# Filler products ahead of and between TensorE's first steps, a rebuilt order search, and a longer run of second stages at the end

## The chip, the cores and the metric

The kernel runs on one core of a Trainium2 chip. The metric is the device time of one execution in microseconds (us). The kernel before was timed in three runs: median 622.8 us, from 619.92 to 622.96.

## What is computed

Attention with a sliding window of 128 positions and 4 sink positions for 4 batches, 8 heads, 768 positions and a head width of 64, and behind it one feed-forward block over the 3072 tokens (512 to 2048 to 512, ELU between).

```python
keep = (pos[None, :] < n_sink) | ((rel >= 0) & (rel < window))
a = softmax(where(keep, scale * q @ k.T, -1e9)); attn = a @ v
x = attn.transpose(0, 2, 1, 3).reshape(B * S, H * D)   # 3072 x 512
h = x @ w_in                                            # 3072 x 2048
g = where(h > 0, h, exp(minimum(h, 0)) - 1)
return g @ w_out                                        # 3072 x 512
```

## The kernel before

The tokens are cut into nine chunks (`SIZES`, line 42) of two or three tiles of 128. Of each chunk the attention is computed first (`attention_f32`, line 545, for chunks 0 and 1 in 32-bit floats; `attention`, line 676, for the others), then the feed-forward block in 16 steps f (`feed_forward`, line 866). Numbers that need it are carried as two 16-bit halves, high and low.

A step f of a chunk has a **first stage** on TensorE (PE): 12 matmuls into one of two PSUM banks h (line 883). Then come an exponential on ScalarE (ACT, line 891), two operations on VectorE (DVE, lines 893 and 896), the high half on ACT (line 897) and the low half on GpSimd (POOL, line 902) or, for chunk 0, on DVE (line 899). The **second stage** on PE takes both halves: three matmuls for each of the chunk's tiles (line 913) into the accumulators. The high and low halves `gh` and `gl` have three buffers each (ring `gh`), so the buffer of step f is written again by step f + 3.

In the attention, scores of two heads (line 586) go through DVE (line 593: mask and row minimum) and ACT (line 596: exponential and sum), are turned on PE (line 603), copied to SBUF by ACT or DVE (line 607), multiplied with the values on PE (lines 644 and 652) and scaled by ACT and DVE (lines 665 to 669). Meanwhile the weights are fetched in 32 pieces and split into halves (lines 325 to 331, 488, 489).

Nothing of this order is left to the tile framework. Every step is a `Task` with an engine, a duration, dependencies and, on PE, a position `pos`. `Plan.order` (line 140) works out due times backwards from the PE positions (`backward`), lets each engine take in simulated time what is ready, PE by position and the others by due time (`forward`), and replays that order five times with small disturbances (`replay`). It does so 64 times, from the fourth on with due times shifted at random by up to 1 us, and keeps the order whose replays end first. `spare` (line 109) adds 1.2 us of slack to every result that another engine hands to a PE task at position 60 or later. A position counts half steps: chunk 8, the last one, begins at 256, and the end (`start`, line 1017) is 288. The plan's end is the end of the last PE task. `keep_order` writes the instructions in the order found; each engine then runs its own in that order.

At the end, the steps f = 13, 14 and 15 of chunk 8 have their second stages split by tile and put behind the last first stage (line 918): the last first stage has position 284.8 (line 886), the second stage of f = 12 has 285. A check follows: DVE reduces the sums of all exponentials (line 1015; the last two steps' at lines 1007 and 1008), PE spreads the result with one matmul at position 286 (line 1017), DVE makes a flag of it (line 1012). Each engine loads the flag (line 1264) and branches on it (line 1265): past a general path, normally not run, to the code that moves the last accumulators out (lines 1273 and 1275) and stores them (line 1276).

At the start, ACT fetches the four words of the scalars, DVE turns them into two numbers (lines 1227 to 1233), and one tiny PE product spreads these over the partitions (line 1234), from which DVE makes the masks.

Of the kernel before, what the change touches and what calls it, by code (L numbers as in the profile page):

```python
# [12 lines left out]
BF16 = mybir.dt.bfloat16  # L13
# [7 lines left out]
P = 128  # L21
B, H, S, D = 4, 8, 768, 64
DM, FF = 512, 2048
# [3 lines left out]
NF = FF // P  # L27
NW = 2 * NF
NS = 4
KW = NS + P  # L30
# [13 lines left out]
HALF = NF // 2  # L44
PARTS = [(0, 0, HALF), (1, 0, HALF), (0, HALF, NF), (1, HALF, NF)] + [(c, 0, NF) for c in range(2, len(SIZES))]
LAG = 2
NEAR = 1
WHOLE = 3
TURNED = 2
# [48 lines left out]
class Plan:  # L98
# [5 lines left out]
    LOADED = 4.3  # L104
    PATIENCE, LEEWAY, ISSUED = 0.1, 5.0, 0.15
    SWITCH = 0.096
    SPARE, SPARE_FROM = 1.2, 60

    def spare(self, t, u):
        return self.SPARE if u.eng == "PE" and t.eng != "PE" and u.pos >= self.SPARE_FROM else 0.0  # L110

    def __init__(self):
        self.tasks, self.rings = [], {}
# [1 line left out]
    def add(self, eng, dur, fn, *args, deps=(), lat=0.0, pos=None, or_=(), gap=2.0, port=None, mode=None):  # L115

        t = Task(eng, dur, fn, args, deps, lat, pos, gap, port, mode)
        for way in or_:
            t.ways[way[0]] = way[1:]
        self.tasks.append(t)  # L120
        return t

    def ring(self, name, writers, users, at=None):

        r = self.rings.setdefault(name, [])
        r.append((writers, users, len(r) if at is None else at))
# [13 lines left out]
    def order(self):  # L140
        self.link()
        pe = sorted((t for t in self.tasks if t.eng == "PE"), key=lambda t: (t.pos, t.n))
        clock = 0.0
        for t in pe:
            t.start = clock
            clock += t.dur
        best, dice = None, random.Random(0)
        for k in range(64):
            self.backward()
            for t in self.tasks:  # L150
                t.due += dice.uniform(-1.0, 1.0) if k >= 3 else 0.0
            self.forward()
            self.tasks.sort(key=lambda t: t.n)
            for i, t in enumerate(sorted(self.tasks, key=lambda t: (t.start, t.n))):
                t.turn = i
            found = [(t.turn, t, t.eng) for t in self.tasks]
            ends = [self.replay(random.Random(i)) for i in range(4)] + [self.replay()]
            end = sum(ends) / len(ends)
            if best is None or end < best[0]:
                best = end, found, {t: t.start for t in self.tasks}  # L160
        self.end = best[0]
        for _, t, e in best[1]:
            t.take(e)
            t.start = best[2][t]
        return [t for _, t, _ in sorted(best[1], key=lambda v: v[0])]

    def replay(self, dice=None):

        order = {e: [] for e in self.HOP}
        for t in sorted(self.tasks, key=lambda t: t.turn):  # L170
            order[t.eng].append(t)
        for e in order:
            order[e].reverse()
        left = {t: len(t.deps) for t in self.tasks}
        ready = dict.fromkeys(self.tasks, 0.0)
        free, dma, lock, mode, last = dict(self.BEGIN), self.LOADED, 0.0, None, 0.0
        for _ in self.tasks:
            _, e = min((max(free[e], ready[o[-1]]), e) for e, o in order.items() if o and not left[o[-1]])
            t = order[e].pop()
            s = max(free[e], ready[t])  # L180
            if e == "PE":
                s, mode = s + (self.SWITCH if t.mode != mode else 0.0), t.mode
                last = s + t.dur
            if t.shares(e):
                s = max(s, lock)
                lock = s + t.dur
            t.start = s
            free[e] = s + t.dur + (0.05 if e == "POOL" else 0.0)
            f = s + t.dur + self.HOP[e]
            if t.lat:  # L190
                dma = max(s + t.dur, dma) + t.lat
                f = dma + t.gap + (dice.choice((-0.5, -0.5, 0.0, 0.5, 1.5)) if dice else 0.0)
            elif dice and e != "PE":
                free[e] += t.dur * dice.uniform(0.0, 0.04)
            for u in t.succ:
                ready[u] = max(ready[u], f if e != "PE" or u.eng != e else s + t.dur)
                left[u] -= 1
        return last
# [183 lines left out]
def fast_path(tc, ctx, first, kq, vx, wt, out, nw, inside, flag, limits):  # L382
# [56 lines left out]
    def slot(name):  # L439
        turn[name] = turn.get(name, -1) + 1  # L440
        return turn[name] % RINGS[name]
# [98 lines left out]
                later.append((writer, us))  # L540
        x_old.append((lo, hi, users))

    later, po_users = [], []

    def attention_f32(c):

# [129 lines left out]
    def attention(c):  # L676
# [10 lines left out]
        def split_keys(h):  # L687


            st = kqs[slot("kqs")]  # L690
            buf = kqr[slot("kq")] if c >= WHOLE else None
            o, kw = KQ_OFF[c, h], kc + qc
            if c < WHOLE:
                ld = None
                if (c, h) not in first["kq"]:
                    ld = add("SP", 0.45, lambda: nc.sync.dma_start(st[:, :kw], kq[:, o : o + kw]), lat=dma_us(P * kw * 4))
                users = []
                return st, None, ld, ld, users
            raw, hi = st[:, :kw], buf[:, :kw]
            ld = None  # L700
            if (c, h) not in first["kq"]:
                ld = add("SP", 0.45, lambda: nc.sync.dma_start(raw, kq[:, o : o + kw]), lat=dma_us(P * kw * 4))
            th = add("ACT", act_us(kw), lambda: nc.scalar.activation(hi, raw, AF.Copy, scale=KQ_SCALE), deps=[ld])  # L703

            lo = buf[:, KQ_MAX : KQ_MAX + kc]
            tk = add("DVE", dve_us(kc), lambda: nc.vector.scalar_tensor_tensor(lo, raw[:, :kc], KQ_SCALE, hi[:, :kc], ALU.mult, ALU.subtract), deps=[th], port=True)
            tl = add("DVE", dve_us(qc), lambda: nc.vector.scalar_tensor_tensor(hi[D:, kc:], raw[D:, kc:], KQ_SCALE, hi[D:, kc:], ALU.mult, ALU.subtract), deps=[th], port=True)  # L707
            users = []
            ring("kqs", [ld or th], [th, tk, tl])
            ring("kq", [th], users)  # L710
            return hi, lo, tk, tl, users

        def taken_values(p, val, prods, v_users, po):
# [152 lines left out]
    def feed_forward(c, f0, f1, start):  # L866
# [4 lines left out]
        for f in range(f0, f1):  # L871
            hp = h_ps[slot("h")]
            gf = gs[slot("g")][:, :n]
            i = slot("gh")
            gh, gl = ghs[i], gls[i]

            def stage1(hp=hp, f=f):
                win = w[2 * f].rearrange("p t (a f) -> p t a f", a=ND)
# [36 lines left out]

            deps = [th, tl, *w_done[2 * f + 1], *(evacs[:nt] + (po_users if c == len(SIZES) - 1 else []) if f == f0 else s2)]
            at2 = start + 2 * (f - f0) + 1 + 2 * LAG
            if c == len(SIZES) - 1 and f >= f1 - 3:

                if len(s2) < nt:  # L920
                    s2 = s2 * nt
                at2 = [start + 2 * (f1 - 1 - f0) + (0.5 + 0.01 * i if f == f1 - 1 else 0.1 * i + 0.01 * f) + (0.0 if i < nt - 1 else 1.0) for i in range(nt)]
                s2 = [add("PE", 3 * 0.216, stage2([(k, i) for k in range(3)]), deps=[th, tl, *w_done[2 * f + 1], s2[i]], pos=at2[i]) for i in range(nt - (f == f1 - 1))] + s2[nt - (f == f1 - 1) :]
                if f == f1 - 1:
                    for e, end in enumerate(ends):
                        s2[-1] = add("PE", 3 * (0.162, 0.057)[e], stage2([(k, nt - 1) for k in range(3)], parts=[end]), deps=[th, tl, *w_done[2 * f + 1], s2[-1]], pos=at2[-1] + 0.001 * e)
            elif f < f1 - 1:
                s2 = [add("PE", 3 * nt * 0.216, stage2([(k, i) for k in range(3) for i in range(nt)]), deps=deps, pos=at2)]
            else:

                s2 = [add("PE", 3 * 0.216, stage2([(k, i) for k in range(3)]), deps=deps, pos=at2 + 0.01 * i) for i in range(nt)]
            ring("g", [a], [b] if near else [th, tl])
            ring("gh", [th], s2)
        for i in range(nt if c < len(SIZES) - 1 else 0):
            rows_ = out[r0 + i * P : r0 + (i + 1) * P, :]
            if f1 < NF:
# [77 lines left out]
    sp = s_ps[len(s_at) % RINGS["s"]]  # L1014
    a = add("DVE", 1.45, in_range, deps=[*seen, *exps_done[:-2], limits_])
    a = add("DVE", 0.2, last_in_range, deps=[a, *exps_done[-2:]])
    b = add("PE", 0.1, lambda: nc.tensor.matmul(sp[:, 0:3], ones, some16, start=True, stop=True), deps=[a], pos=start - 2.0)
    ring("s", [b], [add("DVE", 0.16, decide, deps=[b])], len(s_at))
    for writer, users in later:
        writer.deps.extend(users)  # L1020
    tasks = plan.order()
    if VERBOSE:
        plan.report()
    keep_order(tc, tasks, first["spread"])


VERBOSE = False
# [186 lines left out]
def attention_moe(tc, kq, vx, words_in, wt, out):  # L1214
    nc = tc.nc
    with ExitStack() as ctx:
# [14 lines left out]
        nc.vector.tensor_scalar(nw1, low, 0.0, None, ALU.is_lt)  # L1231
        nc.vector.tensor_tensor(nw1, nw1, high, ALU.add)
        nc.vector.scalar_tensor_tensor(nw1, nw1, 4294967296.0, low, ALU.mult, ALU.add)
        spread = nc.tensor.matmul(last_acc[:, 0:2], ones1, nw1, start=True, stop=True).ins
        nc.vector.tensor_copy(nw, last_acc[:, 0:2])

# [7 lines left out]

        widths = {"kqs": KQ_MAX, "vs": (NK_MAX + 1) * P}
        first = {n: [pool.tile([P, w], F32, name=f"{n}{i}") for i in range(RINGS[n])] for n, w in widths.items()}
        first["spread"] = spread
        first["kq"], first["vs_"] = {(0, 0), (0, 2)}, {(0, 0)}
        nk, qc = len(key_tiles(CHUNKS[0])), len(CHUNKS[0]) * P
        for n, i, src, o, w in (  # L1250
# [50 lines left out]
```

## Time and profile before

| | |
|---|---|
| runs | 619.92, 622.80, 622.96 us |
| profiled execution | 622.7 us |
| its span, first to last instruction | 620.8 us |
| what lies around the span | 1.9 us |
| PE busy | 603.3 us, 97% of the span |
| DVE, ACT, POOL busy | 77%, 70%, 42% |

Every row is of the one profiled execution. Times in a row count from the span's start. A busy share is that of an engine's instructions; register loads, branches and waits are not in it. In a timeline row the bracket says how long the engine had been idle and what released it; in a row of waits, engine, tile and line stand left of the arrow, what was waited for stands right of it, and then come total us, times and the longest. The letter q behind an engine (PEldq) means its sequencer.

### The profile page before, as it was taken

To read this page: it belongs to the slowest core of one execution; us is meant where nothing else is said; L and a number is where in the kernel's file an instruction comes from. 1 tells how busy PE (TensorE), PEld (TensorE's weight loads), DVE (VectorE), ACT (ScalarE), POOL (GpSimd) and SP (SyncE) were. 2 spreads that over 40 slices of the span, in tenths; PEclk is the share of its full clock that TensorE was granted. 3 is DMA by queue.
4 is the path that set the end of the run, shared out by engine and by line. 5 is a ranking of instruction groups with operands and counts; after the bars stand their busy time and mean duration, and the time that the engine had idled before them with its cause. 6 is when DMAs were issued, how large, how long until landed. Compare 5 with 4: busy or idle time off the path is not lost. (4 is left out here: it accounts for less than half of the span.)

```text
span 620.8 us, 13588 instructions
## 1 busy us (share of the span) xinstructions
PE 603.3 (97%) x4587; PEld 365.8 (59%) x4587; DVE 477.8 (77%) x1284; ACT 435.8 (70%) x1236; POOL 262.2 (42%) x510
## 2 busy tenths in 40 slices
PE   7799999999999999999999999999999999999994
PEld 5576666567766565555555565655555565555552
DVE  7899889979989787787788987887888987433231
ACT  5899999877888786776777777766776776332221
POOL 2678787534344434332334444232434443212221
PEclk9899999999999999999999999999999999999998
DMA  8576876939878565483957948586756935410001
GB/s 308 193 285 249 246 230 206 225 93 213 214 172 215 147 156 124 114 212 79 201 134 199 203 105 161 131 225 127 203 130 152 239 49 133 97 52 1 1 0 57
DMA packets 117359, 97.53 MB, mean 157 GB/s; under 512 B 88994, under 2 KB 94370, under 8 KB 117282
## 3 DMA queue, kind: packets, MB, share of 16 engines
q1 hardware_dynamic: 117136, 96.53, 60.8%
q8 instruction: 38, 0.62, 0.4%
q14 instruction: 39, 0.32, 0.2%
q10 hardware_dynamic: 146, 0.07, 0.0%
HBM read 67.99 MB, written 7.34 MB: 121 GB/s over the span
## 5 line engine op out<-in xcount | busy, mean ns | idle before, releaser
L883 PE MATMUL h<-x,w 128*128 128x384 f16 (+1 forms) x1728 | 271.9, 308 | 1.1 <-DVE gl L899 1.0
L883 PEld LDWEIGHTS <-w 128*128 128x128 f16 x1728 | 167.4, 98 | 88.7 <-issue 3.1
L902 POOL TENSOR_TENSOR gl<-g,gh 128x384 f16<-128x384 f32 (+1 forms) x128 | 114.4, 895 | 190.9 <-ACT gh L897 161.0
L913 PE MATMUL acc<-w,gh 128*128 128x512 f16 x576 | 164.6, 379 | 0.1
L913 PEld LDWEIGHTS <-gh 128*128 128x128 f16 x800 | 75.8, 98 | 70.4 <-issue 1.6
L891 ACT ACTIVATE g<-h 128x384 f32<-128x384 f32 (+1 forms) x144 | 64.4, 448 | 71.4 <-PE h L883 61.9
L897 ACT ACTIVATE gh<-g 128x384 f16<-128x384 f32 (+1 forms) x128 | 62.6, 490 | 54.2 <-DVE g L896 53.8
L813 DVE SCALAR_TENSOR_TENSOR pq<-e,st,pq 128x256 f16<-128x256 f32 x160 | 85.5, 560 | 19.7 <-ACT pq L812 18.9
L800 ACT ACTIVATE e<-e,st 128x264 f32<-128x264 f32 x160 | 78.1, 489 | 17.5 <-DVE st L798 17.2
L913 PE MATMUL acc<-w,gl 128*128 128x512 f16 x288 | 87.8, 379 | 0.0
L893 DVE TENSOR_SCALAR g<-g 128x384 f32<-128x384 f32 (+1 forms) x96 | 36.7, 382 | 62.7 <-ACT g L891 61.7
L812 ACT ACTIVATE pq<-e,st 128x256 f16<-128x256 f32 x160 | 70.8, 483 | 8.0 <-DVE st L805 4.5
L896 DVE SCALAR_TENSOR_TENSOR g<-g,h 128x384 f32<-128x384 f32 (+1 forms) x128 | 65.8, 514 | 5.4 <-ACT g L893 4.4
L913 PE MATMUL last_acc<-w,gh 128*128 128x512 f16 (+1 forms) x192 | 69.9, 370 | 0.0
L798 DVE CUSTOM_DVE_ANT_0 e<-s,m 128x264 f32<-128x264 f32 x160 | 61.0, 404 | 11.2 <-PE s L777 10.8
L913 PEld LDWEIGHTS <-gl 128*128 128x128 f16 x400 | 38.5, 98 | 44.5
L804 POOL TENSOR_SCALAR st<-st 128x2 f32<-128x2 f32 x80 | 20.9, 261 | 85.2 <-ACT e L800 81.4
L703 ACT ACTIVATE kq<-kqs 128x780 f16<-128x780 f32 (+1 forms) x48 | 42.7, 897 | 10.5 <-PE s L777 8.1
L489 POOL TENSOR_TENSOR w<-wv,w 128x512 f16<-128x512 f32 x32 | 38.9, 1223 | 5.7 <-ACT w L488 4.6
L776 PE MATMUL s<-kq 128*128 128x264 f16 (+1 forms) x144 | 35.5, 267 | 0.5 <-DVE kq L707 0.5
L777 PE MATMUL s<-kq 128*128 128x264 f16 (+1 forms) x144 | 35.5, 267 | 0.0
L913 PE MATMUL last_acc<-w,gl 128*128 128x512 f16 (+1 forms) x96 | 35.5, 370 | 0.0
(152 smaller groups left out, 817.0 us busy)
## 6 DMA issues: line engine op xcount, KB each, us to landing
raw<-in_wt_dram SPq DMA_DIRECT2D x32, 512.0 KB, 5.1
kqs<-in_kq_dram SPq DMA_DIRECT2D x24, 456.0 KB, 3.5
kqs<-in_kq_dram SPq DMA_DIRECT2D x24, 390.0 KB, 3.4
qk<-in_kq_dram SPq DMA_DIRECT2D x48, 195.0 KB, 4.6
out_dram<-wv SPq DMA_DIRECT2D x21, 256.0 KB, 4.5
vs<-in_vx_dram SPq DMA_DIRECT2D x20, 256.0 KB, 3.1
vm<-in_vx_dram SPq DMA_DIRECT2D x6, 768.0 KB, 5.8
vs<-in_vx_dram SPq DMA_DIRECT2D x12, 320.0 KB, 3.9
```

Source lines behind the costliest of these rows:

```text
L489: tl = add("POOL", 1.16, lambda: nc.gpsimd.tensor_tensor(w[k][:, 1, :], v, w[k][:, 0, :], ALU.subtract), deps=[th])
L703: th = add("ACT", act_us(kw), lambda: nc.scalar.activation(hi, raw, AF.Copy, scale=KQ_SCALE), deps=[ld])
L798: red = add("DVE", 0.08 + 0.00104 * wd, lambda ee=ee, me=me, sp=sps[e], m=m, wd=wd: nc.vector.tensor_tensor_reduce(ee, sp[:, :wd], m[:, :w ...
L800: ex = add("ACT", act_us(wd, sums=True), lambda ee=ee, me=me, rs=rs[:, e : e + 1]: nc.scalar.activation(ee, ee, AF.Exp, bias=me, scale=-1. ...
L812: a = add("ACT", act_us(nb * P, True), lambda src=src, hi=hi, re=re: nc.scalar.activation(hi, src, AF.Copy, scale=re), deps=[rr])
L813: b = add("DVE", dve_us(nb * P) + 0.03, lambda src=src, hi=hi, lo=lo, re=re: nc.vector.scalar_tensor_tensor(lo, src, re, hi, ALU.mult, ALU ...
L883: nc.tensor.matmul(hp[:, :n], win[:, part, d, :], xx[:, :n], start=k == 0, stop=k == 3 * ND - 1)
L891: a = add("ACT", act_us(n) + 0.06, lambda gf=gf, hp=hp, sums=sums: nc.scalar.activation(gf, hp[:, :n], AF.Exp, scale=1.0 / G_SCALE, accum_ ...
L896: b = add("DVE", dve_us(n) - 0.035, lambda gf=gf, gd=gd, hp=hp: nc.vector.scalar_tensor_tensor(gd, gf, 0.0, hp[:, :n], ALU.min, ALU.max), ...
L897: th = add("ACT", act_us(n) - (0.03 if near else 0.0), lambda gd=gd, gh=gh: nc.scalar.activation(gh[:, :n], gd, AF.Copy), deps=[b])
L902: tl = add("POOL", pool_us(n), lambda gl=gl, gd=gd, gh=gh: nc.gpsimd.tensor_tensor(gl[:, :n], gd, gh[:, :n], ALU.subtract), deps=[th])
L913: nc.tensor.matmul(to[:, : cols.stop - cols.start], gg[:, i * P : (i + 1) * P], wout[:, part, cols], start=f == f0 and k == 0, stop=f == f ...
```

## The change

It has four parts. (1) Nine matmuls of 248 columns of ones go to PE ahead of the scalars' spreading product (`EARLY`). (2) After the plan is made, each PE task that the plan starts before 28 us gets such matmuls in front of it, as many as fit the gap that the plan has between it and the PE task before, less 0.2 us, at 0.11 us each; nobody reads their results. The first PE task gets one. (3) The search takes 250 trials instead of 64; from the fourth on a trial starts from the best due times so far and shifts those of one stretch of 25 us that reaches over a gap of PE. The plan's end also counts the flag's end plus 4.5 us (`JUMP`). (4) In chunk 8 the slack of 1.2 us is no longer given from position 274 on; the second stage of f = 12 is split by tile and put behind the last first stage like those of f = 13 to 15, its halves held in two buffers of the keys and queries (`kqr`) that are free by then; the check's matmul has position 285 instead of 286.

```diff
+EARLY, WARM_UNTIL = 9, 28.0
...
-    SPARE, SPARE_FROM = 1.2, 60
+    SPARE, SPARE_POS = 1.2, (60, 2 * NF * len(SIZES) - 14)
+    JUMP = 4.5
     def spare(self, t, u):
-        return self.SPARE if u.eng == "PE" and t.eng != "PE" and u.pos >= self.SPARE_FROM else 0.0
+        return self.SPARE if u.eng == "PE" and t.eng != "PE" and self.SPARE_POS[0] <= u.pos < self.SPARE_POS[1] else 0.0
...
-        for k in range(64):
-            self.backward()
+        for k in range(250):
+            if k < 3:
+                self.backward()
+                due = {t: t.due for t in self.tasks}
+            else:
+                a = dice.choice(best[4]) + dice.uniform(-25.0, -5.0)
+                size = dice.choice((0.5, 1.5, 4.0))
+                due = {t: d + (dice.uniform(-size, size) if a < t.start < a + 25.0 else 0.0) for t, d in best[3].items()}
             for t in self.tasks:
-                t.due += dice.uniform(-1.0, 1.0) if k >= 3 else 0.0
+                t.due = due[t]
...
+    def waits(self):
+        pe = sorted((t for t in self.tasks if t.eng == "PE"), key=lambda t: t.start)
+        return [b.start for a, b in zip(pe, pe[1:]) if b.start - a.start - a.dur > 0.25]
...
+            if not t.succ and e == "DVE":
+                last = max(last, f + self.JUMP)
...
-            i = slot("gh")
-            gh, gl = ghs[i], gls[i]
+            held = c == len(SIZES) - 1 and f == f1 - 4
+            if held:
+                gh, gl = kqr[0][:, :TOK_MAX], kqr[1][:, :TOK_MAX]
+            else:
+                i = slot("gh")
+                gh, gl = ghs[i], gls[i]
...
-            if c == len(SIZES) - 1 and f >= f1 - 3:
+            if c == len(SIZES) - 1 and f >= f1 - 4:
...
-            ring("gh", [th], s2)
+            if held:
+                th.deps.extend(u for us in kq_users[-2 * RINGS["kq"] :] for u in us)
+            else:
+                ring("gh", [th], s2)
...
-    b = add("PE", 0.1, lambda: nc.tensor.matmul(sp[:, 0:3], ones, some16, start=True, stop=True), deps=[a], pos=start - 2.0)
+    b = add("PE", 0.1, lambda: nc.tensor.matmul(sp[:, 0:3], ones, some16, start=True, stop=True), deps=[a], pos=start - 3.0)
...
+    pe = sorted((t for t in tasks if t.eng == "PE" and t.start < WARM_UNTIL), key=lambda t: t.start)
+    pe[0].fn = filled(pe[0].fn, first["warm"], h_ps[1], 1)
+    for a, b in zip(pe, pe[1:]):
+        b.fn = filled(b.fn, first["warm"], s_ps[1] if a.start > 7.0 else h_ps[1], int((b.start - a.start - a.dur - 0.2) / 0.11))
     keep_order(tc, tasks, first["spread"])
+
+def filled(fn, warm, to, n):
+    def run(*args):
+        for _ in range(n):
+            warm(to)
+        fn(*args)
+    return run
...
+        ones_k, ones_n = (nc.const_aps.tensor(1.0, [P, n], BF16) for n in (P, DM - 2 * KW))
+        def warm(to):
+            nc.tensor.matmul(to[:, 2 * KW :], ones_k, ones_n, start=True, stop=True)
+        for _ in range(EARLY):
+            warm(last_acc)
         spread = nc.tensor.matmul(last_acc[:, 0:2], ones1, nw1, start=True, stop=True).ins
```

## Rows read from the trace of the kernel before

**Rows 1.** The page, part 1: busy time of each engine over the span.
```profile
PE 603.3 (97%) x4587; PEld 365.8 (59%) x4587; DVE 477.8 (77%) x1284; ACT 435.8 (70%) x1236; POOL 262.2 (42%) x510
```

**Rows 2.** Busy time by stretch: PE, PEld, DVE, ACT, POOL, clock, DMA share, GB/s.
```profile
8.00:12.00 4.00, 4.00 (x27) 3.11 (x27) 3.16 (x16) 2.89 (x10) 0.57 (x3) 1.00 1.01 393
...
16.00:20.00 4.00, 2.16 (x14) 1.17 (x10) 4.00 (x15) 3.32 (x14) 2.34 (x4) 0.85 0.68 261
20.00:24.00 4.00, 3.88 (x32) 2.63 (x28) 2.68 (x10) 3.01 (x8) 1.51 (x4) 0.72 0.01 2
...
32.00:48.00 16.00, 15.78 (x149) 11.09 (x147) 14.89 (x44) 15.74 (x47) 11.85 (x20) 1.00 0.81 286
...
64.00:128.00 64.00, 62.29 (x466) 40.21 (x467) 56.94 (x140) 57.55 (x168) 44.77 (x71) 1.00 0.84 232
128.00:256.00 128.00, 128.00 (x1039) 81.55 (x1037) 106.34 (x300) 101.48 (x299) 51.14 (x116) 1.00 0.68 160
```

**Rows 3.** Waits of PE over the whole span.
```profile
PE last_acc L1234 <- DVE one_row L1233: 2.7, 1, 2.7
PE h L603 <- ACT e L596: 1.8, 1, 1.8
...
PE h L883 <- DVE gl L899: 1.0, 2, 0.7
```

**Rows 4.** Timeline of PE, first 30 us: start, duration, line, tiles, shape, count.
```profile
7.47 1.54 PE L603 MATMUL h<-ident,e 128*128 128x128 f32 x6
...
12.36 0.87 PE L603 MATMUL h<-ident,e 128*128 128x128 f32 x6
...
19.32 1.25 PE L586 MATMUL s<-kqs 64*128 64x264 f32 x4
...
23.16 0.72 PE L586 MATMUL s<-kqs 64*128 64x264 f32 x4
...
29.26 1.47 PE L883 MATMUL h<-x,w 128*128 128x256 f16 x12
```

**Rows 5.** Waits of DVE that PE ended, first 30 us.
```profile
DVE pt L607 <- PE h L603: 2.4, 3, 1.2
...
DVE e L593 <- PE s L586: 1.3, 3, 0.6
```

**Rows 6.** Timeline of the last 20 us, all engines.
```profile
603.12 0.59 PE L913 MATMUL acc<-w,gh 128*128 128x512 f16 x2
...
605.08 2.11 PE L883 MATMUL h<-x,w 128*128 128x384 f16 x12
...
608.36 0.16 DVE L1008 SCALAR_TENSOR_TENSOR some<-some 128x1 bf16<-128x1 f32 x1
...
609.67 0.92 POOL L902 TENSOR_TENSOR gl<-g,gh 128x384 f16<-128x384 f32 x1 [3.12 <-issue]
...
610.27 0.17 PE L1017 MATMUL s<-some,ones 128*128 128x3 bf16 x1
...
610.50 0.16 DVE L1012 TENSOR_REDUCE words<-s 128x1 int32<-128x3 f32 x1 [1.52 <-PE s L1017]
...
612.84 0.22 PE L913 MATMUL last_end<-w,gl 128*128 128x128 f16 x1
...
615.23 0.69 DVE L1275 TENSOR_SCALAR rows<-acc 128x512 f32<-128x512 f32 x1 [4.56 <-DVEq L1265]
615.83 0.55 DVE L1275 TENSOR_SCALAR rows<-last_acc 128x384 f32<-128x384 f32 x1
```

**Rows 7.** The branch's line 1265 by sequencer: count, duration min/median/max in ns, start.
```profile
L1265 ACTq COMPARE_BRANCH  x1: 50/50/50, 611.2 to 611.2; - x1
...
L1265 PEldq COMPARE_BRANCH  x1: 3322/3322/3322, 611.3 to 611.3; - x1
```

**Rows 8.** DMA queues from 612.0 to 613.1 us: packets, MB, share of 16 engines.
```profile
q14 instruction: 3, 0.02, 7.0%
q8 instruction: 1, 0.02, 5.6%
```

More of the change, by code (lines that the diff above doesn't have):

```diff
@@ L147, in order @@
         best, dice = None, random.Random(0)
-        for k in range(64):
-            self.backward()
+        for k in range(250):
[6 more added lines that the diff above has]
+                due = {t: d + (dice.uniform(-size, size) if a < t.start < a + 25.0 else 0.0) for t, d in best[3].items()}
             for t in self.tasks:
-                t.due += dice.uniform(-1.0, 1.0) if k >= 3 else 0.0
+                t.due = due[t]
             self.forward()
-            self.tasks.sort(key=lambda t: t.n)
             for i, t in enumerate(sorted(self.tasks, key=lambda t: (t.start, t.n))):
@@ L159, in order @@
             if best is None or end < best[0]:
-                best = end, found, {t: t.start for t in self.tasks}
+                best = end, found, {t: t.start for t in self.tasks}, due, self.waits()
         self.end = best[0]
@@ L541, in x_taken @@
         x_old.append((lo, hi, users))
-    later, po_users = [], []
+    later, po_users, kq_users = [], [], []
     def attention_f32(c):
@@ L710, in split_keys @@
             ring("kq", [th], users)
+            kq_users.append(users)
             return hi, lo, tk, tl, users
@@ L1246, in attention_moe @@
         first = {n: [pool.tile([P, w], F32, name=f"{n}{i}") for i in range(RINGS[n])] for n, w in widths.items()}
-        first["spread"] = spread
+        first["spread"], first["warm"] = spread, warm
         first["kq"], first["vs_"] = {(0, 0), (0, 2)}, {(0, 0)}
```

## The prediction

> **What bounds the kernel now.** I read the page first: TensorE is busy for 97% of the span and no other engine for more than 77% [rows 1]. Then the busy time by stretch, to see where the missing 3% lies: from 128 us on PE is busy for 128.00 of 128.00 us, and so it stays until its last product; between 64 and 128 us it loses 1.71 us; the worst stretch is 16 to 20 us, where it works for 2.16 of 4 us while DVE works for all of them [rows 2]. So nothing is to be had between 128 us and the last products except by doing less on PE, and the change adds and removes no useful product. The time can only come from the two ends, and, in a small measure, from the gaps before 128 us.
>
> The waits of PE put names to the start: 2.7 us before the first product, which waits for the scalars, and one gap of 1.8 us until an exponential is done [rows 3]. The timeline of PE shows something that the busy share hides: the same six turning products take 1.54 us at 7.47 and 0.87 us at 12.36, and the same four score products take 1.25 us at 19.32 and 0.72 us at 23.16 [rows 4]. The granted clock falls to 0.85 and 0.72 in the stretches from 16 to 24 us, behind the gap of 1.8 us; there PE ran part of the time at the lower of its two levels, 1.2 instead of 2.4 GHz. The waits of DVE show who felt it: 3.7 us (2.4 and 1.3) of DVE's idle time before 30 us ended with a turning product or a score product [rows 5].
>
> The timeline of the last 20 us shows the other end: PE's last product ends at 613.06, yet DVE moves the first accumulator only at 615.23 and the last one at 615.83 [rows 6]. The view of the branch line shows what lay between: PE's branch took 3.32 us, that of ACT 0.05 [rows 7].
>
> **Part 1 and 2, the fillers.** What they cost: nine matmuls of 248 columns. The nearest row is twelve of 256 columns in 1.47 us at full clock, 0.12 each [rows 4]; at half clock some 0.24, so nine take 1.1 to 2.2 us. They fall into the 2.7 us in which PE waits for the scalars [rows 3], less what the program's opening takes of them; at worst one filler sticks out and the spreading product, and all masks behind it, come 0.2 us later. Those between the tasks cost nothing where the planned gap is real; the gap of 1.8 us would hold (1.8 - 0.2) / 0.11, that is 14, by the code's own rule.
>
> What they bring is a clock that rises earlier and does not fall later. By the two pairs of rows, work at the low level takes 1.7 times as long. From 7.47 to about 12 us PE works without a pause at the low level [rows 2, 4]: 4.5 us that would be 2.6, a gain of 1.9. From 16 to 24 us the clock lacks 0.15 of one stretch of 4 us and 0.28 of the other [rows 2], 1.7 us in all, which is 3.4 us at half clock; these would be 2.0, a gain of 1.4. Together 3.3 us of PE. What of it lies on the path: DVE's waits that PE ended are 3.7 us, so the next engine in line is free to follow for about that much, but from 16 to 20 us DVE has no idle time at all, and from 32 to 48 us ACT is busy for 15.74 of 16 [rows 2, 5]. Whatever is gained before 28 us is kept (both engines simply begin that stretch sooner); what can't be kept is PE time that these two then lack. I take 2.0 of the 3.3 us. The ends are 3.3 us of gain and 0.2 us of loss, the delay of the spreading product.
>
> One reading must be decided here. The clock column says 1.00 for 8 to 12 us, the durations say half [rows 2, 4]. I go by the durations: equal products can't differ by 1.7 otherwise. The Trainium skill, "TensorE: Matmul & The Clock Gate", section "What's actually happening", says the same of the start: the throttled state is the default and activity ends it; its section "Seeing it yourself" warns that clock events in a profile have been unreliable. By the column alone the early part would be worth at most the 1.4 us of the second stretch, and the forecast would be some 1.1 us higher.
>
> **Part 3, the search.** It can remove gaps of PE between 28 and 128 us, of which 1.71 us lie after 64 [rows 2], 1.0 of them waits for the low half on DVE [rows 3]; it can as well deal new ones, since the order of everything changes and the plan's durations aren't the chip's. I take 0, with 2 us either way. Beyond 128 us every wait is covered by slack that stays until position 274.
>
> **Part 4, the end.** PE's work stays the same, so its last product stays at 613.06 less the early gain. What moves is the chain of the check. Now: the second stage of f = 12 runs at 603.12, the last first stage at 605.08, the last sum is judged by 608.52 (3.44 us after that stage's start), the spreading matmul stands behind five of nine tile sets and runs at 610.27, the flag is there at 610.66, and the first accumulator moves 4.57 us later, at 615.23 [rows 6]. With f = 12 behind it and no slack asked, the last first stage takes that place: 603.12 instead of 605.08, 1.96 earlier. The judgement then ends at 606.56; the matmul, one position earlier, waits at most for the set in progress (a third of 1.96, 0.65), and the flag is there at about 607.5, some 3.2 us earlier. PE's own branch comes behind all its products in its queue, and the last of these wait for POOL's low half, which ended at 610.59, 5.51 us after the stage's start [rows 6]; that moves to 608.63. If this wait holds the branch back, the branch moves by 1.96 us and DVE's first move to 613.3; if not, by up to 3.2, but then the last products themselves (613.06) hold the last accumulator, which moves at about 613.1 instead of 615.83: 2.7 us. I take 2.0, the smaller of the two, because PE reads its instructions in order. The four extra buffers and splits cost nothing: the keys' buffers have had their last reader tens of us before, and the nine products of f = 12 stay nine of the same widths (the last tile's in two pieces, as before). The check's matmul without slack can make PE wait; behind it stand all remaining sets, so each 0.1 us costs 0.1 us; DVE's last judgement takes 0.16 us, and I put twice that, 0.3, as the bound of the loss.
>
> The lower end is 0: if PE's branch took 3.32 us because it waited for PE's last product, moving the flag gives nothing. Against that speak the instruction fetches between 612.0 and 613.1 us, three on one queue and one on another [rows 8], that is, begun before PE was done: the branch waits for code. The Trainium skill, "Runtime: NRT & Kernel Launch", section "Instruction fetch mechanics", has that rule: a taken branch out of the code at hand waits for a DMA fetch of its target. By the rule the end is worth 2.0 us, by the other reading 0.
>
> **The sum.** The profiled execution took 622.7 us (span 620.8 and 1.9 around it), 0.1 under the median of 622.8. 622.7 - 2.0 (start) - 0 (search) - 2.0 (end) = 618.7 us.
>
> **The rivals.** The bound of what can be told from no change is 0.5%, 3.1 us: faster is below 619.7, slower above 625.9.
>
> *The end alone.* DVE and ACT swallow the early gain. For it: DVE's 4.00 of 4 and ACT's 15.74 of 16 [rows 2]. Against: DVE's 3.7 us of waits for PE [rows 5]. 620.7 us.
>
> *The start alone.* The branch waits for PE's end. For it: PE's branch ends 1.6 us after PE's last product and only PE's is long [rows 6, 7]. Against: the fetches [rows 8]. 620.7 us.
>
> *The change doesn't do what it says.* The clock rises no sooner, the first stage is not moved: 622.7 us.
>
> *Slower: fillers that outrun their gaps.* Their place is the first 28 us of PE's queue, their number comes from the plan's gaps, and PE can't pass them. Where the plan assumes full-clock durations it believes in 3.3 us of idle time that the chip doesn't have, room for 30 fillers; at half clock these take 30 x 0.24 = 7.2 us, all of it ahead of real products. If the nine first ones do not raise the clock, that is added and the early gain is lost: 622.7 + 7.2 - 2.0 = 627.9 us. It decides with the clock at the first planned gaps: once it is up, a filler fits its 0.11 us and the mechanism is gone. Against it: scores of the first chunk are planned at 1.0 us for four products, close to the low level already (line 588).
>
> **How the numbers follow.** My forecast gets 0.53, the end alone 0.20, the start alone 0.11, nothing 0.07, slower 0.09. Of the forecast, with its 2 us either way from the search, 0.46 lies below 619.7; of the two halves, 0.09 does, when the half that works goes to its upper end (2.7 and 3.3) or the search helps. Faster 0.55, slower 0.09, the same 0.36. The range reaches from both upper ends with a little help of the search (622.7 - 3.3 - 2.7 - 1.2 = 615.5) to the case that nothing happens (622.5).
>
> **What would show it.** Right: the six turning products near 7.5 us at 0.87 instead of 1.54; no fall of the clock before 24 us; the last first stage ahead of f = 12's second stage; the flag over 4 us before PE's last product; DVE's first move within 1 us of that product. Wrong at the start: fillers at 0.2 us each and PE busy with them when data are there; wrong in the middle: new waits of PE after 28 us; wrong at the end: DVE's first move still 2 us behind PE's last product.

## The result, and the profile after

The changed kernel took 616.04 us (median of 5 runs, 615.47 to 616.37), the kernel before in the same session 622.8 (619.92 to 624.79): a ratio of 0.9905, 95% interval 0.988 to 0.993, or 5.9 us (4.4 to 7.5); the two medians lie 6.8 apart. Forecast were 618.7 us and a gain of 4.0. The profiled execution took 615.47 us, the shortest of the five; its span is 613.7 us instead of 620.8.

The stretches of [rows 2] in the changed kernel (PE, PEld, DVE, ACT, POOL, clock, DMA share, GB/s):

```profile
8.00:12.00 4.00, 3.77 (x39) 2.49 (x36) 3.57 (x17) 3.47 (x12) 1.27 (x4) 1.00 0.98 377
...
16.00:20.00 4.00, 3.66 (x34) 2.16 (x32) 4.00 (x14) 4.00 (x15) 3.68 (x7) 1.00 0.94 370
20.00:24.00 4.00, 2.55 (x30) 2.03 (x31) 3.45 (x15) 4.00 (x13) 3.38 (x6) 1.00 0.68 236
...
64.00:128.00 64.00, 63.01 (x481) 42.07 (x480) 56.97 (x146) 59.36 (x172) 43.46 (x69) 1.00 0.76 219
128.00:256.00 128.00, 128.00 (x1098) 81.69 (x1096) 109.40 (x300) 102.02 (x300) 51.55 (x119) 1.00 0.74 164
```

From 16 to 20 us PE stands idle for 0.34 us instead of 1.84, and the clock stays up; from 20 to 24 us it now idles for 1.45 us. From 128 us on PE is without a gap as before. ACT has no pause from 16 to 24 us and DVE none from 16 to 20, so these two seem to bound the start. The timeline of PE at the start, against [rows 4]:

```profile
0.77 2.02 PE L1273 MATMUL last_acc<-const-bfloat16-1.0 128*128 128x248 bf16 x9 [0.77 <-PEq L1335]
2.74 0.58 PE L1277 MATMUL last_acc<-one_row 1*128 1x2 f32 x2
...
7.36 0.87 PE L617 MATMUL h<-ident,e 128*128 128x128 f32 x6
...
23.41 0.59 PE L1273 MATMUL s<-const-bfloat16-1.0 128*128 128x248 bf16 x4 [0.90 <-DVE st L607]
```

The spreading product starts at 2.74, as before, so the nine fillers ahead of it delay nothing. The six turning products at 7.36 take 0.87 us, those of before took 1.54; other executions with the same fillers show less of this (last section). Only twelve fillers stand between tasks. The last row shows something that I had not priced: a filler waits, here 0.90 us, until DVE has read the bank that it writes beside the scores.

The end, against [rows 6]:

```profile
596.88 4.06 PE L902 MATMUL h<-x,w 128*128 128x384 f16 x24
...
600.78 0.81 PE L932 MATMUL acc<-w,kq 128*128 128x512 f16 x3
...
602.33 0.16 PE L1039 MATMUL s<-some,ones 128*128 128x3 bf16 x1
...
602.74 0.15 DVE L1034 TENSOR_REDUCE words<-s 128x1 int32<-128x3 f32 x1
...
606.61 0.60 ACT L1316 ACTIVATE rows<-acc 128x512 f32<-128x512 f32 x1 [3.23 <-DVEq L1308]
...
606.68 0.69 DVE L1318 TENSOR_SCALAR rows<-acc 128x512 f32<-128x512 f32 x1 [3.79 <-DVEq L1308]
...
608.80 0.22 PE L932 MATMUL last_end<-w,gl 128*128 128x128 f16 x1
608.96 0.56 DVE L1318 TENSOR_SCALAR rows<-last_acc 128x384 f32<-128x384 f32 x1 [1.58 <-PE last_acc L932]
```

The last two first stages run back to back, the four second stages (`kq` holds those of f = 12) behind them. The flag is there at 602.89, 6.1 us before PE's last product ends at 609.02 (before: 2.4 us). The first accumulators move at 606.6, while PE still multiplies, and the last one as soon as its product is there. Who branched when, against [rows 7] (flag load on line 1307, branch on line 1308):

```profile
L1308 ACTq COMPARE_BRANCH  x1: 50/50/50, 603.5 to 603.5; - x1
...
L1308 ACTq EVENT_SEMAPHORE  x1: 17/17/17, 606.5 to 606.5; - x1
...
L1308 PEldq COMPARE_BRANCH  x1: 4122/4122/4122, 607.5 to 607.5; - x1
```

```profile
L1307 ACTq TENSOR_LOAD <-words x1: 470/470/470, 602.9 to 602.9; - x1
...
L1307 PEldq TENSOR_LOAD <-words x1: 486/486/486, 606.9 to 606.9; - x1
```

ACT branched at 603.5 and went on at 606.5, a microsecond before PE even took its branch at 607.5. So the span shrank by 7.1 us in two places: PE's last product came 4.0 us earlier (613.06 to 609.02), and from there to the last instruction it took 4.7 us instead of 7.7. These are figures of one execution each.

### The profile page after: what moved, and what is told of

The parts are those of the page before. It is cut to its first block, busy times and chain, and to the rows that moved or that the text cites. A ratio compares the mean times of both kernels' runs of the same rounds, so it can differ in the third digit from the quotient of the medians.

```text
span 613.7 us, 13669 instructions
## 1 busy us (share of the span) xinstructions
PE 603.9 (98%) x4608; PEld 365.2 (60%) x4608; DVE 480.3 (78%) x1284; ACT 435.1 (71%) x1236; POOL 263.5 (43%) x510
## 4 chain that ended last, share of the span: by engine, by line
PE 87%; DVE 6%; ACT 5%; issue 1%; POOL 0%; ACTq 0%; DVEq 0%
PE h L902 37%; PE acc L932 27%; PE last_acc L932 10%; PE s L791 2%; PE s L792 2%; PE last_end L861 2%; PE s L861 2%; ACT last_acc L339 1%; DVE wv L345 1%; DVE e L607 1%; ACT g L910 1%; DVE wu L343 1%; ACT w L502 1%; DVE pt L621 1%; ACT gh L916 1%
```

## The experiments

The change has three parts that can be had apart: fillers, search, end. All eight combinations were measured. First come four kernels built from the changed one:

**No fillers.** `EARLY = 0`, and the loop that wraps the tasks left out.

> The changed kernel without any filler: neither the nine nor those between tasks; plan, order and end are the changed kernel's. Theory: the earlier clock is worth most of what the start gained, so the first turning products near 7.5 us again take about 1.5 us instead of 0.87, PE's last product comes 2.0 to 3.2 us later (near 611 to 612 instead of 609.0) and the time is 618 to 619.3. Rival (the new order made the start shorter, the clock is a bystander): within 0.5 us of the changed kernel, 615.5 to 616.5. If the clock is also what makes runs differ from each other, the runs spread over 2 us or more, against 0.9 with fillers.

Measured: 617.52 us (9 runs, 616.14 to 618.17), ratio 0.9928 (0.9905 to 0.9951) to the kernel before on the same chip. PE's last product ended at 610.49, 1.5 later than with fillers. Less than the theory's 2.0, more than the rival's 0.5: the fillers are worth about 1.5 us here, and most of the 4.0 us by which PE's last product moved is not their doing. The runs spread over 2.0 us; since kernels with fillers later spread as far, that says nothing of the clock.

That the clock is what brings the 1.5 us is not shown. Both kernels run the same instructions in the same order on every engine, so first stages can be compared one by one (timelines of PE, first without fillers, then the changed kernel):

```profile
25.07 1.48 PE L902 MATMUL h<-x,w 128*128 128x256 f16 x12
...
67.94 0.83 PE L902 MATMUL h<-x,w 128*128 128x256 f16 x6
...
119.89 1.47 PE L902 MATMUL h<-x,w 128*128 128x256 f16 x12 [0.87 <-DVE g L915]
```

```profile
25.02 1.48 PE L902 MATMUL h<-x,w 128*128 128x256 f16 x12
...
67.80 1.05 PE L902 MATMUL h<-x,w 128*128 128x256 f16 x8
...
118.42 1.47 PE L902 MATMUL h<-x,w 128*128 128x256 f16 x12
```

At 68 us the changed kernel leads by no more than 0.14 us, at 120 us by 1.47. In between, PE of the kernel without fillers waited for DVE, 0.25 us at 69.67 and 0.87 us at 119.89, waits that the changed kernel doesn't have. They come 40 us and more behind the last filler; where they come from was not tried.

**The nine alone**, and **the twelve between tasks alone** (`EARLY = 0`).

> The nine products ahead of the spreading product alone, no fillers between tasks. If the nine raise the clock and PE's own work keeps it up: full clock from about 7 us, 616.0 us, the same as the changed kernel within 0.5. If the twelve between the tasks are needed to raise it or to hold it: the clock rises later or falls again in the first 28 us and the time is 617 to 618.5.

> The twelve fillers between tasks alone, without the nine at the start. If the nine are what raises the clock: the products near 7.5 us take about 1.5 us again, time 617.5 to 619. If the fillers between tasks do it: 616.0 within 0.5.

Measured: 616.13 (6 runs, ratio 0.9907, 0.9874 to 0.994) and 615.51 (6 runs, 0.9898, 0.9865 to 0.993). Each half brings the time that both bring, so neither is needed if the other is there. But the nine alone did so without the earlier clock that was expected of them, at least in the execution profiled (616.94 us): the turning products at 7.54 still took 1.54 us. Its first stages, in the same order again:

```profile
26.17 1.05 PE L902 MATMUL h<-x,w 128*128 128x256 f16 x8
...
119.65 1.47 PE L902 MATMUL h<-x,w 128*128 128x256 f16 x12
```

They begin 1.1 us behind those of the kernel without fillers and are 0.2 us ahead of them at 120 us, since the two waits for DVE are not there. PE's last product ended at 610.25. In the profiled execution of the twelve alone the turning products took 1.35 us, and PE's last product ended at 609.10.

**The old end**, with fillers and new search:

```diff
-    SPARE, SPARE_POS = 1.2, (60, 2 * NF * len(SIZES) - 14)
-    JUMP = 4.5
+    SPARE, SPARE_POS = 1.2, (60, 10**9)
+    JUMP = 0.0
...
-            held = c == len(SIZES) - 1 and f == f1 - 4
+            held = False
...
-            if c == len(SIZES) - 1 and f >= f1 - 4:
+            if c == len(SIZES) - 1 and f >= f1 - 3:
...
-    ..., deps=[a], pos=start - 3.0)
+    ..., deps=[a], pos=start - 2.0)
```

> The changed kernel with the end of before: three second stages behind the last first stage, slack of 1.2 us kept to the end, the check's matmul at position 286, the flag not counted in the plan's end; fillers and new search stay. Theory: the end of the change is worth about 3.1 us, all of it after PE's last product: from that product's end to the last instruction it takes 7.7 us again instead of 4.7, and the time is 619. Rival (the end was worth only the 2.0 us that I forecast, the rest of the gain came from the order): 618, with PE's last product moved too.

Measured: 618.65 (12 runs, 0.9951, 0.9931 to 0.9971), 2.9 us more by the ratios. Its timeline at the end:

```profile
606.75 0.16 DVE L1034 TENSOR_REDUCE words<-s 128x1 int32<-128x3 f32 x1 [1.52 <-PE s L1039]
...
609.09 0.22 PE L932 MATMUL last_end<-w,gl 128*128 128x128 f16 x1
611.38 0.69 DVE L1318 TENSOR_SCALAR rows<-acc 128x512 f32<-128x512 f32 x1 [4.47 <-ACTq L1308]
```

PE's last product ended at 609.31, only 0.3 later than in the changed kernel; the first accumulator moved 2.1 us behind it, and the span of 617.4 us ends 8.1 behind it. The theory holds: the end is worth about 3 us, all behind PE's last product.

The other four combinations follow. **The old search** (64 trials, as in the diff's removed lines):

> The changed kernel with the search of before (64 trials, every due time shifted at random by up to 1 us); fillers and end stay as changed. The kernel without fillers took 617.5 and the one with the old end 618.7 against 616.0, which leaves about 1.5 us of the 5.7 gained over the 621.7 of the same chip for the search. If the parts simply add: 617.5. If the search is worth nothing by itself: 616.0. If fillers and search do the same thing (either of them closes the gap of 1.8 us in which the clock fell): 616.0 to 616.5 as well, but with the clock held up and a long gap of PE between 12 and 24 us in the trace.

Measured: 621.23 (12 runs, 0.9985, 0.9958 to 1.0011). None of the three expectations: without the new search, fillers and end together bring nothing that can be measured. **Fillers alone**, **search alone** and **end alone**, each with the two other parts as before:

> The kernel before, its order and its end, with the fillers alone: nine at the start and those that its own plan has room for. If parts add: 621.7 - 1.5 = 620.2. If fillers are worth more in the old order, because there the clock also fell a second time: 618.5 to 619.5, with no fall between 12 and 28 us. If they only delay: 622 or more.

Measured: 620.43 (12 runs, 0.9973, 0.9952 to 0.9994), as if the parts added. The gap in which the clock fell is still there, since the plan has no gap at that place and so puts nothing into it (timeline of PE, and the clock in the eighth number of the stretches):

```profile
17.20 0.44 PE L613 MATMUL h<-ident,e 128*128 128x128 f32 x2 [1.84 <-ACT e L606]
...
18.76 1.07 PE L654 MATMUL last_end<-pt,vm 128*64 128x128 f32 x8
```

```profile
16.00:20.00 4.00, 2.80 (x26) 2.14 (x26) 3.97 (x20) 3.73 (x14) 1.08 (x4) 0.83 0.69 267
20.00:24.00 4.00, 4.00 (x36) 2.61 (x32) 2.89 (x10) 3.05 (x10) 2.36 (x4) 0.74 0.17 29
```

> The kernel before with the new search alone, no fillers, the old end. If parts add: 621.7 - 1.5 = 620.2, and from PE's last product to the last instruction 7.7 us or more as before. If the new order by itself keeps the clock from falling the second time, as in the run without fillers: 619.5 to 620. If the search is worth nothing: 621.7.

Measured: 619.91 (12 runs, 0.9977, 0.9955 to 0.9999), and the clock does not fall a second time, as the second expectation has it. Until the last steps the order is that of the kernel without fillers: the new search, with this seed, found the same order for both ends. Even so the earliest first stage begins at 26.07 here and at 25.07 there (timeline of PE), and PE's last product ended at 611.36 and 610.49:

```profile
26.07 1.16 PE L902 MATMUL h<-x,w 128*128 128x256 f16 x9
```

The trace's records of the clock tell these two executions apart: the first record, at full speed, lies at 12.0 us here and at 10.0 us there (the clock column prints 1.00 ahead of the first record too). By these two executions a clock that is up 2 us sooner is worth about 0.9 us in this order, the lead lasts to the end, and it can come without a filler. A still earlier clock brought no more: in the changed kernel that record lies at 7.2 us, and its earliest first stage begins at 25.02.

> The kernel before with the new end alone: four second stages behind the last first stage, no slack from position 274, the check one position earlier, the flag counted in the plan's end; old search, no fillers. Theory: 2.6 to 3.4 us less than before on the same chip, about 618.7, with 4.7 to 5.3 us from PE's last product to the last instruction. Rival (the forecast's step: PE's branch holds the others back): 2.0 us less, 619.7.

Measured: 621.87 (12 runs, 0.9998, 0.9977 to 1.0018): no gain at all. The end did its part, 4.8 us from PE's last product to the last instruction; but that product ended at 615.88, 2.8 us later than before. The old search, given another end, had dealt another order for everything, with PE idle for 4.0 us where the order of before left 1.7 (against [rows 2], and the waits that made it, against [rows 3]):

```profile
64.00:128.00 64.00, 59.98 (x446) 38.91 (x443) 56.57 (x132) 57.01 (x163) 42.90 (x69) 0.97 0.76 214
```

```profile
PE h L898 <- DVE g L911: 2.2, 1, 2.2
PE h L898 <- DVE gl L914: 1.7, 3, 0.9
```

The clock of 0.97 in this row is a fall behind the longest of these waits (0.79 from 72 to 80 us), which cost a further 1.7 us. The kernel with fillers and end has the same order and the same two rows of waits, but its clock stayed up:

```profile
64.00:128.00 64.00, 60.02 (x455) 39.40 (x453) 57.95 (x138) 57.32 (x165) 43.90 (x70) 1.00 0.78 221
```

Put together (PE's last product and what follows it, from the profiled executions; us saved by the ratios, of 622):

```
fillers search end   saved   PE's last product ends   from there to the last instruction
   -      -     -     0            613.1                 7.7
   x      -     -     1.7          611.0                 7.8
   -      x     -     1.4          611.4                 7.3
   -      -     x     0.1          615.9                 4.8
   x      x     -     3.0          609.3                 8.1
   x      -     x     0.9          613.2                 5.5
   -      x     x     4.5          610.5                 5.2
   x      x     x     5.9          609.0                 4.7
```

Each saving is uncertain by 1.2 to 1.7 us either way. Read by PE's last product, fillers bring 1.5 to 2.7 us wherever they are added. The two kernels of each such pair run in one order, and their first stages show where the lead arises. At 68 us it is 1.6 us with nothing else changed, 0.7 with the new search, 0.9 with the new end and 0.14 with both. The rest comes between 68 and 131 us: 1.7 us of it with the new end alone through the fall of the clock told above, and some 1.3 us in both pairs of the new search where the kernel without fillers waits for DVE. The last column changes with the end alone, by 2.1 to 3.4 us. The search brings 1.7 us with the old end and 4.2 to 5.4 with the new one, because there it also makes good the bad draw.

**Is the new search better, or luckier?** Two more seeds of it, one more of the old search (fillers and new end in all), and 750 trials instead of 250:

> The changed kernel with another seed of its search (1 instead of 0). Theory: the stepwise search finds a good order reliably; 615.5 to 617, PE idle for about 1 us between 64 and 128 us. Rival: the 5 us between the changed kernel and the same with the old search are one lucky draw; then this lands anywhere from 616 to 621.

> As the run before it, with seed 2: 615.5 to 617 by the theory, 616 to 621 by the rival.

> Fillers and end as changed, the old search with seed 1 instead of 0. Theory: the old search leaves 2 us or more of PE idle between 64 and 128 us whatever the seed; 618.5 to 622. Rival (seed 0 was an unlucky draw of the old search): 616 to 617.5, with 1 to 1.7 us idle there.

> The changed kernel with 750 trials of its search instead of 250. If the plan's end still tells the chip's: 614.5 to 615.5, the gain lying before 128 us, since PE has no gap behind it and the end can't get shorter (4.7 us from PE's last product). If the search has run into what the plan's durations can tell: 616.0 within 0.5, or worse.

Measured, against 621.03 for the kernel before: 616.57 (6 runs, 0.9926, 0.9904 to 0.9947), 620.0 (12 runs, 0.9978, 0.9961 to 0.9994), 616.95 (6 runs, 0.9929, 0.9909 to 0.9949) and 615.95 (6 runs, 0.9915, 0.9894 to 0.9936). The rival holds: of three draws of the new search one keeps only 1.4 us of the 5.9, of two draws of the old search one comes within 1.5 us of the changed kernel by the ratios. PE's idle time between 64 and 128 us is no sign of it: 1.6, 1.7, 0.7 and 0.95 us in these four. Five draws don't tell the two searches apart. More trials bring nothing that can be told. No run beats the changed kernel beyond its interval.

The poor draw, seed 2, shows the slower rival at work, at full clock (timelines of PE, DVE and ACT):

```profile
22.11 1.68 PE L1273 MATMUL s<-const-bfloat16-1.0 128*128 128x248 bf16 x14 [1.51 <-DVE st L607]
23.72 0.44 PE L658 MATMUL last_end<-pt,sv 128*64 128x128 f32 x4
...
25.61 1.15 PE L1273 MATMUL s<-const-bfloat16-1.0 128*128 128x248 bf16 x9
```

```profile
25.55 0.42 DVE L680 TENSOR_TENSOR rx<-last_end,rx 128x256 f32<-128x256 f32 x1 [2.34 <-ACT rx L679]
```

```profile
25.14 0.38 ACT L679 ACTIVATE rx<-last_end 128x256 f32<-128x256 f32 x1 [1.79 <-PE last_end L666]
```

Fourteen fillers waited 1.51 us for DVE to leave their bank and then ran for 1.6 us ahead of value products, while DVE and ACT stood still for want of those; nine more followed. How much of this draw's 4 us is the fillers' and how much the order's was not tried.

## Why the prediction was right, and where it was off

- **Range and sign held**; the gain was 5.9 us, not 4.0. The places were right: nothing behind 128 us, one gain before, one behind PE's last product. How near the time came is partly luck of the draw: with the other two seeds the same change saves 4.6 and 1.4 us.
- **Fillers, forecast 2.0.** Measured 1.5 to 2.7 by PE's last product, 0.8 to 1.7 by the ratios. The reading of the durations against the clock column was right: the six turning products went from 1.54 to 0.87 us while the column shows 1.00 in both. The trace's first record of full clock agrees, at 12.0 us before and at 7.2 us in the changed kernel. The step "Whatever is gained before 28 us is kept" held: in the old order the fillers gained 1.2 us by the earliest first stage and 2.0 by PE's last product. In the new order they gained only 0.05 to 0.6 us by the earliest first stage, and most of their worth arose behind 68 us, where the prediction had none. Wrong was the detail that fillers would fill the gap of 1.8 us, "14, by the code's own rule": the rule knows the plan's gaps, not the chip's, and in the old order put nothing there. The gap went with the new order, and with it the second fall of the clock, fillers or not.
- **Search, forecast 0 with 2 us either way.** This is the term that was mis-sized: 1.4 to 1.7 us by itself, 4.2 to 5.4 between this draw and the old search's draw for the new end. I had priced the search as the removal of gaps between 28 and 128 us. With the end of before nothing was gained there; PE idles 1.0 us less before 28 us, and the clock stays up. With the new end the larger part did lie there: PE's idle time between 64 and 128 us goes from 4.0 us to 2.1 without fillers and to 1.0 with them. That under the old search an edit of the end alone deals another order for everything, with PE's last product 2.8 us later, I had not priced. By its seed alone the new search moves the time by some 4 us.
- **End, forecast 2.0.** The step that failed is "I take 2.0, the smaller of the two, because PE reads its instructions in order". PE loaded the flag only at 606.9, 4.0 us after it was there, but nobody waits for PE: ACT and DVE load and branch for themselves and were at work on the first accumulators before that. The upper case, 2.7 us, was the right one: 2.9 us by the ratios, 2.1 to 3.4 by the profiles. The lower reading, that moving the flag gives nothing because the branch waits for PE's last product, is refuted by the same rows; whether PE's own branch, which ended 2.6 us behind that product, waits for it stays open. The fetch of code stands: three instruction packets follow the branches of ACT, DVE and SP about a microsecond later, as in [rows 8], and each of these engines goes on about 3 us after its branch. The Trainium skill, "Runtime: NRT & Kernel Launch", section "Instruction fetch mechanics", states that a taken branch to code not yet at hand waits for a DMA fetch of it, and this trace agrees.
- **The check's matmul without slack, at most 0.3.** PE was idle for 0.09 us there.
- **The slower rival, 0.09.** Not in this draw, where the scores behind the filler that waited 0.90 us start at 24.37, and at 24.42 without fillers. Its mechanism showed in another draw, and not where I put it: at full clock, through the fillers' wait for a bank.

Packets by queue from 604.4 to 605.3 us in the changed kernel:

```profile
q14 instruction: 3, 0.02, 9.4%
```

## What to carry to other kernels

Where an order is found by a seeded search, an edit's effect is the edit plus a new draw: compare marks that the draw can't move (here the time behind PE's last product), and measure several seeds before the search or the edit is credited. Kernels that run in one order can be compared step by step, and that shows where a gain arises; here it was not where the fillers stand. Products that only keep the clock up belong where the chip is idle, not where the plan is, and into a bank that no one else reads. If a branch with a far target stands ahead of the last stores, have its condition ready some 4 us before the last product: in these runs DVE's first move came 3.8 to 4.6 us after the flag.

## What I had not expected of the hardware

The flag was ready at 602.9, but PE loaded it at 606.9, when 17 products were still to start. In all ten kernels with the new end it is 17 products, 4.0 us behind the flag; in the four with the old end 14 were to start, and PE loaded it at once (before: at 610.7). Which limit stands behind that was not tried.

With the same kind of fillers between the tasks, the clock does not come up at the same time. The six turning products took 0.87 us in the changed kernel's profiled execution alone and 1.33 to 1.54 in the eight others with such fillers; in the five without, the nine alone among them, they took 1.54. The first record of full clock lies at 7.2 to 10.9 us in the nine kernels with fillers between the tasks and at 10.0 to 12.2 us in the five without, at 12.2 with the nine alone. So the fillers between the tasks bring the clock forward, mostly by less than the profile of the changed kernel shows.
